# Later stores of converted weight tiles: five slots behind the operations that make them, tied to a product

## The chip, the cores and the metric

The kernel runs on one core of a Trainium2 chip. The metric is the device time of one execution in microseconds (us), as a median of runs. Five engines run side by side: TensorE (PE, matrix products; PEld is its weight load), VectorE (DVE), ScalarE (ACT), GpSimd (POOL) and SyncE (SP). SP computes nothing here. It issues almost all transfers between the chip's memory (HBM) and the on-chip memory, one after the other: its queue is in order, and an issue that has to wait for its data holds up everything queued behind it.

## What is computed

Eight batches of causal attention with two kinds of masks (four heads look at the last 32 positions, four at every 32nd position), then a feed-forward layer with the gate h * cos(h). All data are float32.

```python
scores = np.where(masks, scale * np.matmul(q, k.transpose(0, 1, 3, 2)), -1e9)   # (8, 8, 576, 576)
attn = np.exp(scores - np.max(scores, axis=-1, keepdims=True))
attn = attn / (np.sum(attn, axis=-1, keepdims=True) + 1e-09)
x = np.matmul(attn, v).transpose(0, 2, 1, 3).reshape(4608, 512)
h = x @ w_in                       # w_in 512 x 2048, float64 on input
g = h * np.cos(h)
return g @ w_out                   # w_out 2048 x 512, float64 on input
```

The weights arrive as 64-bit numbers, and the kernel itself turns them into 32-bit ones.

## The kernel before

There are two long stages. In the first, to about 490 us, the attention of batch b + 1 is worked in between the products of batch b with w_in, and h goes to HBM (`h_all`). In the second, h comes back in pairs of tiles, passes the gate and is multiplied by w_out. Every operand is split into a high and a low part, and a product of two is three products of parts.

**Slots.** The first stage has 8 x 56 slots of the program. The weights w_in stand as 8 blocks f, and a block in a batch is seven products by a scheme with seven in place of eight, in 7 slots (`STEP`); 8 blocks make the 56 slots of a batch (`PER_BATCH`). Each product is six matmuls (L532). A dictionary `plan` says which product is begun in which slot, `bursts` where units of attention are worked in, and `steps` what else is traced there. PE's order is written out by hand: `in_turn` orders each matmul behind the one before.

**What follows a product.** PE's results are combined in `hidden` (L550 on DVE, L548 on ACT) into a buffer of h, of which there are three (pool `hb`). When both halves are there, L552 stores the buffer with SP. By the order of the products a store of h falls to the slots 5 and 6 of every seven, one of each of two neighbouring blocks. So the stores come in pairs, and they tell in the timeline of SP which slot is being worked. A buffer is free again when its store has landed, and DVE works its queue in order: the operations of the next softmax stand behind an L550 that waits for a buffer.

**The conversion of w_out.** `whole_output_weights` treats tile n of 16. `land` (L156) loads 512 KB of 64-bit words into a tile `raw`, of which there are three. In slot 112 + 17 n, `to_float32` works it with two operations of ACT (L165, L169) and two of DVE (L170, L173) into the tile `sums`, of which there is one, and L583 stores that to `w_all` in HBM. `output_sums` treats the four pairs f = 1, 2, 4, 5 (`SEVEN`) in slots 112 + 17 (2 f + 2) and 8 later. It loads a pair of tiles of `w_all` into a tile of the ring `raw` (L602), makes four sums and differences of quarters in another tile of the ring with three operations of POOL (the last is L610), and stores them to `t_all` with L611. Later `output_weights` and `split_sums` read `w_all` and `t_all` back, split them and keep them for the second stage.

**Who sets the order.** A planner puts each engine's instructions in a row by a simulated course of the kernel: an instruction whose inputs and buffers are ready there is placed then. `with_product(i)` adds an edge without a semaphore: in the plan, instruction i comes no earlier than the last matmul that was traced before it. On the chip the tie itself makes nothing wait. Generators make the steps: `in_steps(work, *slots)` continues the generator `work` in each of the slots given, up to its next `yield`.

Of the kernel before, what the change touches and what calls it, by code (L numbers as in the profile page):

```python
# [100 lines left out]
def attention_cos_ffn(ctx, tc, qkl, vl, qkvs, w_in, w_out, eye, eye16, mask_l0, mask_l, mask_s, out):  # L101
    nc = tc.nc
# [19 lines left out]
    w_all = dram.tile([NFC, P, DM], F32, name="w_all")  # L122
    t_all = dram.tile([len(SEVEN), P, 2 * DM], F32, name="t_all")
# [9 lines left out]
    def order(later, first, reason):  # L133
        tc.add_manual_dep(
            later.ins, first.ins.name,
            mybir.DependencyInfo(mybir.DependencyClass.NoSync, mybir.DependencyReason.DATA), reason=reason,
        )
# [12 lines left out]
    def with_product(begun):  # L150
        if turn is not None:
            order(begun, turn, "with this product")

    def land(cv, src):
        raw = cv.tile([P, 512, 2], I32, name="raw", bufs=3)
        load = nc.sync.dma_start(out=raw.rearrange("p n w -> p (n w)"), in_=src)  # L156
        if len(loads) == UNITS:
            order(load, loads[-1], "units first")
        return raw

    def to_float32(raw, out, bits=None):
        low, top = raw[:, :, 0], raw[:, :, 1]
        scaled = top.bitcast(F32)
        bits = low if bits is None else bits
        with_product(nc.scalar.activation(  # L165
            out=bits, in_=low.bitcast(U32), func=AF.Copy, scale=2.0 ** -29 * (1.0 - 2.0 ** -16),
            bias=7.5 * 2.0 ** -16 - 0.5,
        ))
        with_product(nc.scalar.activation(out=scaled, in_=scaled, func=AF.Copy, scale=2.0 ** -112))  # L169
        nc.vector.scalar_tensor_tensor(  # L170
            out=bits, in0=top, scalar=-0x80000000, in1=bits, op0=ALU.bitwise_and, op1=ALU.bitwise_or
        )
        nc.vector.scalar_tensor_tensor(  # L173
            out=out, in0=top, scalar=3, in1=bits, op0=ALU.logical_shift_left, op1=ALU.bitwise_or
        )
# [402 lines left out]
    def whole_output_weights(cv, n):  # L578
        raw = land(cv, w_out.bitcast(I32)[n])
        yield  # L580
        t = cv.tile([P, 3, 2 * P], F32, name="sums")[:, :2].rearrange("p k n -> p (k n)")
        to_float32(raw, t.bitcast(I32))
        nc.sync.dma_start(out=w_all[n], in_=t)  # L583
        yield

    def output_weights(room, n, rest=nc.gpsimd):
# [8 lines left out]
    def whole_tile(cv):  # L595
        return cv.tile([P, 512, 2], I32, name="raw", bufs=3).bitcast(F32).rearrange("p n w -> p (n w)")

    def output_sums(cv, n):

        f = SEVEN[n]  # L600
        both = whole_tile(cv).rearrange("p (f n) -> p f n", f=2)
        nc.sync.dma_start(out=both, in_=w_all[2 * f:2 * f + 2].rearrange("f p n -> p f n"))  # L602
        yield
        b = both.rearrange("p f (j n) -> p (f j) n", j=2)
        t = whole_tile(cv).rearrange("p (j n) -> p j n", j=4)
        with_product(nc.gpsimd.tensor_tensor(
            out=t[:, :2], in0=b[:, 1:2].broadcast_to([P, 2, 2 * P]), in1=b[:, 0:4:3], op=ALU.subtract
        ))
        nc.gpsimd.tensor_tensor(out=t[:, 2], in0=b[:, 3], in1=t[:, 0], op=ALU.subtract)
        nc.gpsimd.tensor_tensor(out=t[:, 3], in0=b[:, 2], in1=t[:, 2], op=ALU.subtract)  # L610
        nc.sync.dma_start(out=t_all[n], in_=t.rearrange("p j n -> p (j n)"))  # L611
        yield

    def split_sums(room, n):
# [161 lines left out]
    with ExitStack() as phase:  # L776
        cv = phase.enter_context(tc.tile_pool(name="cv", bufs=1))
# [16 lines left out]
        m, n, o = ((pools[name], name) for name in "mno")  # L794
# [58 lines left out]
        def in_steps(work, *slots):  # L853
            work = iter(work)
            for slot in slots:
                steps.setdefault(slot, []).append(partial(next, work, None))

        for n in range(2, NF):
            for i in range(2):
                at = 7 * n + 7 * i // 2 - 13  # L860
# [2 lines left out]
            in_steps(weight_sums(cv, f), *(16 + 10 * f + i for i in (0, 2, 5, 7)))  # L863
        for n in range(NFC):
            at = 2 * PER_BATCH + 17 * n
            in_steps(whole_output_weights(cv, n), at - 10, at)
        for n in range(NFC - LATE):
            at = (B - 1) * PER_BATCH + STEP * (n // 2) + 12 + 3 * (n % 2)
            in_steps(output_weights(lambda: whole_tile(cv)[:, :DM], n), at - 6, at)
        for n, f in enumerate(SEVEN):  # L870
            at = 2 * PER_BATCH + 17 * (2 * f + 2)
            in_steps(output_sums(cv, n), at, at + 8)
        for n, at in enumerate(SUMMED):
            at += (B - 1) * PER_BATCH
            in_steps(split_sums(lambda: whole_tile(cv), n), at - 6, at, at + 4)
        for b in range(1, B):
            for i, (summed, made) in enumerate(PREPARED):
                at = (b - 1) * PER_BATCH
# [5 lines left out]
        for slot in range(max(*plan, *steps) + 1):  # L884
            b, at = divmod(slot, PER_BATCH)
# [149 lines left out]
```

## Time and profile before

| | |
|---|---|
| median of 3 runs | 871.63 us (871.21 to 871.90) |
| profiled execution | 872.13 us, its span 870.40 us |
| busy in the span | PE 98%, PEld 91%, DVE 64%, ACT 60%, POOL 60% |
| granted clock of TensorE | 1.00 (2.4 GHz) over the span |
| moved by DMA | 150.22 MB, 173 GB/s on average |

Times are in us from the start of the span. PE's matmuls overlap and their ends are modelled, so its busy share tells where it stood still rather than how near it is to its peak. "L552" is line 552 of the kernel. An entry of the timeline ends with the idle time before it and what ended that.

### The profile page before, as it was taken

What the parts mean: (1) busy time and instruction counts of PE and PEld (TensorE: products, weight loads), DVE (VectorE), ACT (ScalarE), POOL (GpSimd) and SP (SyncE); (2) the same over time, 40 slices, a digit from 0 to 9 for tenths busy, and PEclk for the clock granted to TensorE, in tenths of its full rate; (3) what the DMA queues carried; (4) which work ended last, traced back from release to release, by engine and by line L of the source; (5) the groups of instructions that cost most, each with busy time, mean ns of one, the idle gap of its engine ahead of it and who ended that gap; (6) DMA issues with size and microseconds to landing.
All of it is one profiled execution on the core that took longest, in us unless ns stands there. A gap on an engine that the chain in (4) does not pass through costs nothing.

```text
span 870.4 us, 22827 instructions
## 1 busy us (share of the span) xinstructions
PE 857.0 (98%) x9021; PEld 792.4 (91%) x9021; DVE 554.2 (64%) x1069; ACT 519.6 (60%) x1029; POOL 523.1 (60%) x514
## 2 busy tenths in 40 slices
PE   9899999999999999999999999999999999999998
PEld 5799899999999899999999889999999999999996
DVE  5888756658566566686433666666666666666661
ACT  3766444545345354453456887777777777777772
POOL 2578974416216134171166488888888888888851
PEclk9999999999999999999999999999999999999999
DMA  9698445554766666674355744444444444444430
GB/s 332 206 301 267 144 147 161 191 192 158 265 215 207 231 221 220 211 251 159 129 188 214 250 133 124 131 123 131 124 122 129 126 123 129 130 130 132 134 97 25
DMA packets 91339, 150.22 MB, mean 173 GB/s; under 512 B 8416, under 2 KB 52960, under 8 KB 91232
## 3 DMA queue, kind: packets, MB, share of 16 engines
q1 hardware_dynamic: 90512, 148.54, 52.6%
q8 instruction: 71, 1.16, 0.6%
q14 instruction: 36, 0.29, 0.1%
q10 hardware_dynamic: 720, 0.23, 0.1%
HBM read 95.25 MB, written 53.48 MB: 171 GB/s over the span
## 4 chain that ended last, share of the span: by engine, by line
PE 86%; DMA 4%; DVE 3%; POOL 3%; ACT 2%; issue 2%; SPq 0%; DVEq 0%; POOLq 0%; ACTq 0%
PE q L709 41%; PE m L532 18%; PE n L532 9%; PE m L503 5%; PE o L532 4%; PE acc L331 2%; PE acc L396 2%; PE acc L313 2%; DMA h_all<-h 1%; PE acc L366 1%; PE acc L383 1%; POOL x_lo L179 1%; POOL g_lo L179 1%; DMA both<-w_all 1%; DVE h L550 1%
## 5 line engine op out<-in xcount | busy, mean ns | idle before, releaser
L709 PE MATMUL q<-w,g_hi 128*128 128x512 f32 (+1 forms) x1028 | 215.6, 349 | 0.0
L709 PEld LDWEIGHTS q<-w,g_hi 128*128 128x128 f32 x1028 | 171.1, 189 | 25.5
L179 POOL TENSOR_TENSOR g_lo<-g,g_hi 128x896 fp32r<-128x896 f32 x64 | 135.2, 2134 | 0.2 <-ACT g_hi L178 0.2
L709 PE MATMUL q<-w,g_lo 128*128 128x512 f32 (+1 forms) x514 | 119.4, 349 | 0.3 <-POOL g_lo L179 0.3
L532 PE MATMUL m<-x_hi,w 128*128 128x288 f32 x448 | 109.8, 300 | 1.7 <-DVE h L550 1.0
L532 PE MATMUL m<-x_hi,v 128*128 128x288 f32 x448 | 108.8, 297 | 0.1
L657 ACT ACTIVATE wave<-r,quarter 128x512 f32<-128x512 f32 x144 | 98.6, 685 | 3.3 <-DVE r L655 3.2
L709 PEld LDWEIGHTS q<-w,g_lo 128*128 128x128 f32 x514 | 87.9, 189 | 12.9 <-POOL g_lo L179 0.5
L655 DVE SCALAR_TENSOR_TENSOR r<-wave,h_in 128x512 f32<-128x512 int32 x144 | 95.6, 681 | 4.5 <-ACT wave L654 3.0
L179 POOL TENSOR_TENSOR g_lo<-r,g_hi 128x512 fp32r<-128x512 f32 x44 | 57.1, 1298 | 65.6 <-PE q L709 50.5
L654 ACT ACTIVATE wave<-h_in 128x512 int32<-128x512 f32 x144 | 82.9, 590 | 0.4 <-DMA h_in<-h_all 0.4
L178 ACT CAST g_hi<-g 128x896 fp32r<-128x896 f32 x64 | 60.6, 947 | 36.7 <-PE q L709 29.9
L532 PEld LDWEIGHTS m<-x_hi,w 128*128 128x128 f32 x448 | 78.0, 188 | 3.5 <-DVE h L550 1.7
L532 PEld LDWEIGHTS m<-x_hi,v 128*128 128x128 f32 x448 | 78.0, 188 | 0.5 <-ACT m L540 0.4
L540 ACT COPY m<-m 128x288 f32<-128x288 f32 x112 | 44.6, 398 | 56.1 <-PE m L532 48.6
L283 POOL TENSOR_TENSOR pn_s<-e_sb,z 128x324 f32<-128x324 f32 x28 | 20.9, 746 | 87.2 <-DVE z L281 76.8
L283 POOL TENSOR_TENSOR e_sb<-e_sb,z 128x384 f32<-128x384 f32 x24 | 20.4, 851 | 86.3 <-DVE z L281 77.6
L709 PE MATMUL q<-v,g_hi 128*128 128x256 f32 x512 | 71.9, 283 | 0.0
L532 PE MATMUL m<-x_lo,w 128*128 128x288 f32 x224 | 66.1, 295 | 0.0
L532 PE MATMUL m<-x_lo,v 128*128 128x288 f32 x224 | 66.1, 295 | 0.0
L709 PEld LDWEIGHTS q<-v,g_hi 128*128 128x128 f32 x512 | 66.0, 192 | 0.0
L673 DVE TENSOR_TENSOR g<-wave,h_in 128x512 f32<-128x512 f32 x64 | 44.1, 689 | 28.7 <-ACT wave L657 26.8
(137 smaller groups left out, 2036.5 us busy)
## 6 DMA issues: line engine op xcount, KB each, us to landing
h_all<-h SPq DMA_DIRECT2D x128, 288.0 KB, 2.5
h_in<-h_all SPq DMA_DIRECT2D x144, 256.0 KB, 2.8
qk<-in_qkvs SPq DMA_DIRECT2D x28, 324.0 KB, 4.4
out<-o SPq DMA_DIRECT2D x35, 256.0 KB, 2.7
qk<-in_qkl SPq DMA_DIRECT2D x21, 416.0 KB, 4.4
raw<-in_w_in SPq DMA_DIRECT2D x16, 512.0 KB, 4.5
raw<-in_w_out SPq DMA_DIRECT2D x16, 512.0 KB, 5.2
v<-in_vl SPq DMA_DIRECT2D x24, 224.0 KB, 4.2
```

The source lines that it names most:

```text
L178: with_product(cast(out=hi, in_=x))
L179: return rest.tensor_tensor(out=lo, in0=x, in1=hi.bitcast(F32), op=ALU.subtract)
L283: nc.gpsimd.tensor_tensor(out=pn, in0=e, in1=z[:, :n].unsqueeze(2).broadcast_to([P, n, w]), op=ALU.mult)
L313: self.scored = self.pe(nc.tensor.matmul(s_ps[quarter_of(c), t * KW:(t + 1) * KW], q_t[half(j), p, QB * t:QB * (t + 1)], k_t[half(j), p, Q ...
L503: in_turn(nc.tensor.matmul(self.banks[i, j], a[:, c * P:(c + 1) * P], y[:, c], start=k == 0 and m == 0, stop=k == 1 and m == len(ops) - 1, ...
L532: in_turn(nc.tensor.matmul(bank, a[:, c * P:(c + 1) * P], y[:, c], start=first and i == 0, stop=i == len(ops) - 1, skip_group_check=True,))
L540: nc.scalar.copy(out=t, in_=self.bank[name[0]])
L654: with_product(nc.scalar.activation(out=k, in_=h, func=AF.Copy, scale=1.0 / (2.0 * math.pi), bias=0.25))
L655: nc.vector.scalar_tensor_tensor(out=r, in0=k, scalar=-2.0 * math.pi, in1=h, op0=ALU.mult, op1=ALU.add)
L657: sin = nc.scalar.activation(out=wave, in_=r, func=AF.Sin, bias=quarter)
L673: nc.vector.tensor_tensor(out=g[:, :4].rearrange("p n t -> p (n t)"), in0=wave, in1=h, op=ALU.mult)
L709: in_turn(nc.tensor.matmul(at, a, w, start=first, stop=True, skip_group_check=True))
```

## The change

Both stores get a step of their own: after a `yield`, tied to the last product that was traced when this step comes. The step of the w_all store is 5 slots behind that of the conversion. The step of the t_all store is 5 slots behind that of the sums, which itself stays where it was, 8 slots after slot 112 + 17 (2 f + 2), while the load of the pair moves by one slot.

```diff
@@ whole_output_weights
         to_float32(raw, t.bitcast(I32))
-        nc.sync.dma_start(out=w_all[n], in_=t)
+        yield
+        with_product(nc.sync.dma_start(out=w_all[n], in_=t))
         yield
@@ output_sums
         nc.gpsimd.tensor_tensor(out=t[:, 3], in0=b[:, 2], in1=t[:, 2], op=ALU.subtract)
-        nc.sync.dma_start(out=t_all[n], in_=t.rearrange("p j n -> p (j n)"))
+        yield
+        with_product(nc.sync.dma_start(out=t_all[n], in_=t.rearrange("p j n -> p (j n)")))
         yield
@@ the steps
         for n in range(NFC):
             at = 2 * PER_BATCH + 17 * n
-            in_steps(whole_output_weights(cv, n), at - 10, at)
+            in_steps(whole_output_weights(cv, n), at - 10, at, at + 5)
         for n, f in enumerate(SEVEN):
             at = 2 * PER_BATCH + 17 * (2 * f + 2)
-            in_steps(output_sums(cv, n), at, at + 8)
+            in_steps(output_sums(cv, n), at + 1, at + 8, at + 13)
```

## Rows read from the trace of the kernel before

**Rows 1.** Part 1 of the page: busy time of each engine, its share of the span, instructions.

```profile
PE 857.0 (98%) x9021; PEld 792.4 (91%) x9021; DVE 554.2 (64%) x1069; ACT 519.6 (60%) x1029; POOL 523.1 (60%) x514
```

**Rows 2.** The chain that ended last in order of time: start, length, what. The runs of 24 products of L396, one in each batch of the first stage from the second on.

```profile
121.63 0.84 PE acc L396 x24
...
178.74 0.84 PE acc L396 x24
...
236.63 0.84 PE acc L396 x24
...
294.48 0.84 PE acc L396 x24
...
352.87 0.84 PE acc L396 x24
...
409.91 0.84 PE acc L396 x24
```

**Rows 3.** The timeline of PE: start, length, line, operation, tiles, and in brackets the idle time before it and what ended it. The matmuls between 160 and 430 us for which it marks such a time.

```profile
209.71 0.40 PE L532 MATMUL m<-x_hi,w 128*128 128x288 f32 x1 [0.58 <-DVE h L550]
...
293.42 0.40 PE L532 MATMUL n<-x_hi,w 128*128 128x288 f32 x1 [1.22 <-DVE h L550]
...
351.81 0.40 PE L532 MATMUL n<-x_hi,w 128*128 128x288 f32 x1 [1.02 <-DVE h L550]
```

**Rows 4.** The timeline of DVE: one operation of the conversion of tile 3, and the last of that of tile 7.

```profile
207.36 1.93 DVE L170 SCALAR_TENSOR_TENSOR raw<-raw 128x512 int32<-128x512 int32 x1
...
276.31 0.85 DVE L173 SCALAR_TENSOR_TENSOR sums<-raw 128x512 int32<-128x512 int32 x1
```

**Rows 5.** The timeline of DVE: the four longest stops between 200 and 430 us that the landing of a store of h ended.

```profile
224.46 0.46 DVE L550 TENSOR_TENSOR h<-o,m 128x288 f32<-128x288 f32 x1 [2.24 <-DMA h_all<-h]
...
253.64 0.46 DVE L550 TENSOR_TENSOR h<-o,m 128x288 f32<-128x288 f32 x1 [3.04 <-DMA h_all<-h]
...
289.75 0.46 DVE L550 TENSOR_TENSOR h<-o,m 128x288 f32<-128x288 f32 x1 [3.94 <-DMA h_all<-h]
...
345.39 0.46 DVE L550 TENSOR_TENSOR h<-o,m 128x288 f32<-128x288 f32 x1 [2.84 <-DMA h_all<-h]
```

**Rows 6.** The chain that ended last in order of time: the two stores of h on it between 160 and 430 us (start, time to landing).

```profile
282.72 6.93 DMA h_all<-h
...
340.17 5.10 DMA h_all<-h
```

**Rows 7.** DMA issues by line: out<-in, engine, how many, KB each, median us from issue to landing.

```profile
h_all<-h SPq DMA_DIRECT2D x128, 288.0 KB, 2.5
...
raw<-in_w_out SPq DMA_DIRECT2D x16, 512.0 KB, 5.2
...
w_all<-sums SPq DMA_DIRECT2D x16, 256.0 KB, 2.2
...
t_all<-raw SPq DMA_DIRECT2D x4, 512.0 KB, 3.6
```

**Rows 8.** Waits of SP's queue: line, what it waited for, us in total, times, the longest.

```profile
SPq L583 <- DVE sums L173: 27.3, 11, 6.1
...
SPq L583 <- DVE z L281: 8.5, 3, 4.9
...
SPq L611 <- POOL raw L610: 6.0, 2, 5.4
...
SPq L602 <- DMA w_all<-sums: 4.3, 3, 1.6
```

**Rows 9.** The timeline of ACT: a copy that completes a buffer of h, and the first operation of the conversion of tile 7.

```profile
210.81 0.40 ACT L548 COPY h<-m 128x288 f32<-128x288 f32 x1 [0.60 <-PE m L532]
...
273.55 0.68 ACT L165 ACTIVATE raw<-raw 128x512 int32<-128x512 uint32 x1
```

**Rows 10.** The timeline of SP's queue: start, length, line, transfer, how many in a row (x2: two issues and the time between them).

```profile
211.56 0.38 SPq L552 DMA_DIRECT2D h_all<-h  x1
...
276.64 0.33 SPq L611 DMA_DIRECT2D t_all<-raw  x1
277.01 0.43 SPq L156 DMA_DIRECT2D raw<-in_w_out  x1
277.56 1.39 SPq L552 DMA_DIRECT2D h_all<-h  x2
279.06 0.42 SPq L583 DMA_DIRECT2D w_all<-sums  x1
279.55 2.07 SPq L156 DMA_DIRECT2D raw<-in_w_out  x2
...
282.72 2.15 SPq L552 DMA_DIRECT2D h_all<-h  x2
...
338.36 0.33 SPq L611 DMA_DIRECT2D t_all<-raw  x1
338.74 0.42 SPq L156 DMA_DIRECT2D raw<-in_w_out  x1
340.17 1.21 SPq L552 DMA_DIRECT2D h_all<-h  x2
```

**Rows 11.** Two stretches: start and end, length, busy time of each engine (and instructions), granted clock, DMA share, GB/s.

```profile
276.60:289.70 13.10, 13.10 (x217) 12.58 (x216) 4.79 (x12) 4.07 (x12) 1.88 (x3) 1.00 0.95 328
338.30:345.30 7.00, 7.00 (x137) 6.70 (x136) 2.52 (x7) 3.09 (x8) 0.76 (x2) 1.00 0.95 311
```

## The prediction

> **What bounds the kernel now.** First the busy shares: TensorE (PE) works through 98% of the span [rows 1], so time can only be won where PE stands still, and the change touches one stretch, from the first conversion of w_out to the last, about 158 to 419 us. Second the chain of work in order of time. The same run of 24 products of L396 comes round once per batch, so the distances between their starts are the lengths of the batches [rows 2]: 57.11, 57.89, 57.85, 58.39 and 57.04 us. The first and the last of these five hold conversions and stores too and still take 57.1, so 57.05 is the undisturbed length, and the three between lose 0.84 + 0.80 + 1.34 = 2.98 us. That is all that this stretch has to give: 0.34% of the kernel. Third the timeline of PE for the places of that loss [rows 3]: 0.58 us idle at 209.71, 1.22 at 293.42, 1.02 at 351.81, together 2.82 of the 2.98, each ended by L550 on VectorE (DVE).
>
> What made L550 late differs. At 209.71 DVE itself was slow: the conversion's L170, an operation of 512 elements per partition, took 1.93 us there [rows 4]; no store is in that chain. At 293.42 and 351.81 DVE stood for 3.94 and 2.84 us on "h_all<-h", that is, a buffer of h was not free because its store had not landed [rows 5]; the chain names those stores, issued at 282.72 and 340.17 and landed after 6.93 and 5.10 us [rows 6], where the median is 2.5 [rows 7]. Everything queued behind L550 on DVE, the softmax steps of the next unit among it, waits with it. So the path here is: a full DMA queue, a late h store, a blocked DVE, an idle PE. Not every block reaches PE: DVE stood 3.04 us before 253.64 and 2.24 before 224.46 [rows 5], and the timeline of PE marks no idle time at either.
>
> **What SP waits for.** The queue's own waits [rows 8] put 27.3 + 8.5 us on the stores of L583 and 6.0 on those of L611: SP stands at a store until DVE or GpSimd (POOL) has made its tile. These 41.8 us look like the prize and are not. SP does nothing but issue, so such a wait costs what stands behind it and is already due. After the longest of them, 6.1 us before 211.14, the next entry is an h store at 211.56 [rows 10], whose copy L548 began at 210.81 and took 0.40 [rows 9]: held for 0.35 us. After the 5.4 us before 276.64 comes a load of raw at 277.01 [rows 10]. Of the three buffers of raw one is t itself, one is under conversion until L173 ends at 277.16 [rows 4], so the load takes the third, the pair that the same POOL operations read, and could not go before them in any order.
>
> **The change, part by part.** (1) The 16 stores of w_all (256 KB each) and the 4 of t_all (512 KB) [rows 7] are tied to a product five slots after the step that makes their tile. No instruction is added or removed on any engine; the tie orders the plan alone and sets no semaphore. A batch of 56 slots takes 57.05 us, so a slot is 1.02 us and five are 5.1. But the old stores didn't issue at the step: they wait for the conversion, whose operations take some 3.6 us (the one that L583 stores at 279.06 ran from L165 at 273.55 to the end of L173 at 277.16 [rows 4, 9]). So a store moves by 5.1 - 3.6 = 1.5 us, or 2 with the spread of such times, in SP's plan, past one or two h stores or a pair of q/k and v loads, not by five slots.
>
> (2) Of the 41.8 us of waiting nearly all goes at the stores, yet where a load of raw stood right behind, it takes the wait over, since it needs the same tile free. Worth nothing on the path: 0, with 0 and -0.35 as ends (the time that the h store of 211.56 was held).
>
> (3) At 338.36 the t_all store, and at 338.74 a raw load, go into the queue just ahead of the pair of h stores at 340.17 [rows 10]. In the kernel's slots that pair is of 292 and 293, and the t_all store moves from 290 plus its operations to the product of 295: behind the pair. The queue was full in that stretch, 311 GB/s with the DMA engines 95% busy [rows 11], so 524,288 bytes fewer ahead of the h store are worth 524,288 / 311,000 = 1.69 us of its landing: 343.6 in place of 345.3. That is more than the 1.02 us PE lost there, so all 1.02 should go; ends 0 and -1.34 (that batch's whole excess). I take -1.0.
>
> The Trainium skill, "DMA: Bandwidth & Descriptors", section "Queues, rings and completion order", says that all DMAs that SP issues share one row of rings and each engine consumes a ring in order. The rows agree, an h store taking 2.5 us at the median and 6.93 behind loads, and it speaks against this change: bytes are moved in the queue, none is taken out. By the same page's limit of 358 GB/s (section "Specifications") the 512 KB would be an estimated 1.46 us instead of 1.69, and the sum the same.
>
> (4) The stop before 293.42 should stay. Ahead of the h store of 282.72 stand, from 276.64 on, t_all, three loads of raw, two h stores and one of w_all [rows 10], in a stretch 95% busy at 328 GB/s [rows 11]. After the change t_all is tied to slot 227 and w_all to slot 236, and that h store belongs to the product of 236 and needs its result copied first: both are still ahead. SP still can't pass 276.6, since the raw load there needs POOL's tile. The same bytes from the same start: 0, with ends -1.22 (a raw load slips behind the h store) and +0.8 (another 256 KB gets ahead: 262,144 / 328,000).
>
> (5) The four loads of a pair of w_all tiles (L602) wait for the landing of the store (4.3 us of SP's waits already, [rows 8]), and the raw loads that take their buffer in turn follow them. They shift by the same 1.5 to 2 us. Nothing needs their data at once: the pair is used a dozen microseconds later. But a megabyte, 3.3 us at 311 GB/s, moves closer to other h stores. Ends 0 and +1.22 (the dearest stop shown) at one place; I take +0.3. Moving L602 by one slot keeps its place behind the conversion of the same slot: 0.
>
> (6) Ring of raw tiles: t is held until a store that issues about 2 us later has landed. The next raw loads run many slots ahead of their conversions, so 0. The tile "sums" is written next 12 slots after the moved store: 0. The stage behind 430 us is untouched: 0.
>
> **Sum.** The profiled execution took 872.13 us, its span of 870.40 and 1.73 around it: 872.13 - 1.0 + 0.3 = 871.4. That execution is 0.50 above the median of the runs, 871.63; against the median it is 870.9.
>
> **The rivals.** R1, both jams go: the t_all store, and with its later landing one or two raw loads, fall behind the h store of 282.72 as well. Then 1.22 + 1.02 = 2.24 go, 869.4; with the whole excess of the three batches 868.65. For it: the 6.93 us hang on an order of SP that the plan may well reshuffle. Against: step 4, equal bytes from an equal start. Chance 0.20.
>
> R2, slower: the jam moves to other h stores. The stores now stand directly ahead of the h store of the same product in several cases (slots 117, 236 and 321), and L602 with its raw load ahead of a pair that had them further off. It decides from where DVE is stopped for about 3 us: 2.84 and 3.94 cost PE 1.02 and 1.22, 3.04 cost nothing [rows 3, 5]. Two new such stops with the old ones left: 871.63 + 2 x 1.22 = 874.1. Against: at 3.3 us per megabyte a jam clears within half of the 7 slots (7.1 us) from one pair of h stores to the next, so it must hit them exactly. Chance 0.14.
>
> R3, nothing: the raw loads take over the waits, the t_all store stays ahead of the pair of 340.17 because the plan runs ahead of the chip, and the same bytes stand in the same places: 871.6. Chance 0.21.
>
> My forecast, one of two stops gone and a little given back, has 0.45, with 870.2 to 871.5 as its own range.
>
> **How the numbers follow.** 0.2% (1.74 us) is about what a measurement of this kernel can tell from no change. Below 869.9 lie nearly all of R1 and a small tail of the forecast: 0.23. Above 873.4 lies most of R2, with the shuffling of other queues that no row prices: 0.13. The rest, 0.64, is within. For 8 in 10 the range reaches into R1 and towards R2: 869.0 to 872.9.
>
> **What would show it.** SP's waits at the two store lines should fall from 41.8 us to under 10, with waits at the raw loads' line rising. The t_all store near 338 should come after the h pair, whose first store then lands within about 3.5 us, and the batch of 58.39 us should shorten to about 57.3. The batch with the stop at 293 should stay at 57.85, and the idle time at 209.7 should stay. I'm wrong if a new idle time of PE of a microsecond appears behind a stop of DVE on h_all (R2), if the stop at 293 goes (R1), or if the time moves outside this stretch.

## The result and the profile after

| | before | after |
|---|---|---|
| median | 871.76 us (6 runs, 871.21 to 872.65) | 877.49 us (6 runs, 876.88 to 883.13) |
| profiled execution | 872.13 us, span 870.40 | 877.40 us, span 875.6 |
| PE busy | 857.0 us | 857.7 us |

The change makes the kernel slower: ratio 1.0082, 95% interval 1.0064 to 1.0101. Two executions among the experiments below, the profiled one of the w_all part alone and one of the t_all part alone, ran at a granted clock of 0.66 and took 1175 and 1176 us, and stand in none of the medians and ratios. PE has the same work, so the 5.2 us of span are time in which it stood still or ran slowly. The marks of [rows 2] tell where: in the chain in order of time of the changed kernel (start, length, what) the same runs of L396 stand at

```profile
120.92 0.84 PE acc L396 x24
...
178.01 0.84 PE acc L396 x24
...
241.36 0.84 PE acc L396 x24
...
299.13 0.84 PE acc L396 x24
...
358.01 0.84 PE acc L396 x24
...
415.58 0.84 PE acc L396 x24
```

So the batches take 57.09, 63.35, 57.77, 58.88 and 57.57 us, against 57.11, 57.89, 57.85, 58.39 and 57.04 before. One batch is 5.46 us longer and the last two some 0.5 each; the first mark stands 0.71 us earlier than before, and another half microsecond comes back behind the last.

In that batch the timelines of PE and of DVE and the chain show one new stop of PE, at a place where DVE already stood before (2.24 us, [rows 5]) and PE next to nothing. PE and DVE of the changed kernel (last column: idle time before, and what ended it):

```profile
229.47 0.43 PE L532 MATMUL m<-x_hi,v 128*128 128x288 f32 x1 [4.12 <-ACT m L540]
```

```profile
227.70 0.46 DVE L550 TENSOR_TENSOR h<-o,m 128x288 f32<-128x288 f32 x1 [6.22 <-DMA h_all<-h]
```

The chain there (start, length, what):

```profile
217.98 9.60 DMA h_all<-h
...
228.16 0.41 DVE e_sb L276
...
228.66 0.04 ACT e_sb L277
...
229.04 0.39 ACT m L540
...
229.47 1.63 PE m L532 x6
231.10 1.44 PE o L532 x6
232.54 1.10 PE acc L331 x48
```

It is the mechanism of [rows 5, 6] at a third place: a store of h, of slot 173, lands after 9.60 us, and DVE can't begin L550 nor the softmax step L276 behind it. ACT's L277 waits for L276, and behind L277 in ACT's queue stands the copy L540 that empties the bank `m` for which PE waits. Then a second loss follows: PE begins again at half clock. Busy times in the window behind the stop (start and end, length, PE, PEld, DVE, ACT, POOL, granted clock, DMA share, GB/s):

```profile
229.40:235.00 5.60, 5.53 (x112) 5.12 (x113) 3.22 (x9) 0.94 (x4) 3.42 (x4) 0.70 0.34 118
```

A mean of 0.70 is a stretch at the lower of the two levels (1.2 GHz) after four idle microseconds, and then the upper again. The same three groups took 1.06, 0.79 and 0.83 us before; two of them in the chain of the kernel before:

```profile
226.22 1.06 PE m L532 x6
...
228.08 0.83 PE acc L331 x48
```

So the clock cost 0.57 + 0.65 + 0.27 = 1.49, and 4.12 + 1.49 = 5.61 us is the batch's loss within 0.15.

PE did lose a little at this place before. The timeline of PE marks idle time only above 0.15 us, but these two neighbours in the kernel before leave 0.14 between them (225.79 + 0.29 = 226.08):

```profile
225.79 0.29 PE L532 MATMUL m<-x_hi,w 128*128 128x288 f32 x1
226.22 0.40 PE L532 MATMUL m<-x_hi,v 128*128 128x288 f32 x1
```

So DVE stood 2.24 us for 0.14 of PE before, and 6.22 for 4.12 after: 2.10 us of slack both times.

What stands ahead of the late store is told by SP's queue. Before:

```profile
214.79 0.32 SPq L552 DMA_DIRECT2D h_all<-h  x1
215.20 0.39 SPq L602 DMA_DIRECT2D raw<-w_all  x1
215.64 0.49 SPq L156 DMA_DIRECT2D raw<-in_w_out  x1
216.22 0.38 SPq L358 DMA_DIRECT2D v<-in_qkvs  x1
216.70 0.38 SPq L303 DMA_DIRECT2D qk<-in_qkl  x1
218.26 1.41 SPq L552 DMA_DIRECT2D h_all<-h  x2
```

After:

```profile
210.51 3.87 SPq L552 DMA_DIRECT2D h_all<-h  x2
214.43 0.42 SPq L584 DMA_DIRECT2D w_all<-sums  x1
214.95 0.40 SPq L358 DMA_DIRECT2D v<-in_qkvs  x1
215.44 0.40 SPq L303 DMA_DIRECT2D qk<-in_qkl  x1
216.97 0.38 SPq L603 DMA_DIRECT2D raw<-w_all  x1
217.41 0.47 SPq L156 DMA_DIRECT2D raw<-in_w_out  x1
217.98 0.96 SPq L552 DMA_DIRECT2D h_all<-h  x2
```

The w_all store of tile 3 moved from 211.14 behind the h stores of slots 166 and 167. The load of the first pair reads that tile, so it waits for the landing (2.5 us, to 216.9), and the raw load takes its buffer behind it. The megabyte that left at 215.2 to 215.6 now leaves at 217.0 to 217.4, half a microsecond ahead of the h store, and the moved store's 256 KB are new ahead of it as well. The two loads of v and qk (L358, L303) stand ahead of the h store in both kernels; they only changed places with the megabyte.

The waits of SP (us in total, times, longest) against [rows 8]:

```profile
SPq L613 <- POOL raw L611: 5.4, 1, 5.4
...
SPq L603 <- DMA w_all<-sums: 4.3, 3, 1.6
SPq L156 <- DMA t_all<-raw: 4.0, 2, 3.8
SPq L584 <- DVE sums L173: 3.8, 4, 1.9
SPq L584 <- DVE z L281: 3.2, 1, 3.2
SPq L156 <- DVE sums L173: 2.1, 1, 2.1
```

The waits at the two store lines (L613 and L584) fell from 41.8 to 12.4 us, which is what the edit does by itself; the two rows of the raw loads (L156) hold 6.1 us. No time came of it.

### The profile page after: what moved, and what is told of

Its sections match the earlier page's. It is cut to its first block, busy times and chain, and to the rows that moved or that the text cites. A ratio compares the mean times of both kernels' runs of the same rounds, so it can differ in the third digit from the quotient of the medians.

```text
span 875.6 us, 22827 instructions
## 1 busy us (share of the span) xinstructions
PE 857.7 (98%) x9021; PEld 793.2 (91%) x9021; DVE 553.8 (63%) x1069; ACT 519.9 (59%) x1029; POOL 523.1 (60%) x514
## 4 chain that ended last, share of the span: by engine, by line
PE 84%; DMA 6%; DVE 4%; ACT 2%; issue 2%; POOL 2%; SPq 0%; DVEq 0%; ACTq 0%; POOLq 0%
PE q L711 43%; PE m L532 16%; PE n L532 8%; PE m L503 5%; PE o L532 4%; DMA h_all<-h 4%; PE acc L331 2%; PE acc L396 2%; PE acc L313 1%; PE acc L366 1%; POOL x_lo L179 1%; DVE h L550 1%; PE acc L383 1%; DMA w_all<-sums 1%; DMA v<-in_qkl 1%
## 5 line engine op out<-in xcount | busy, mean ns | idle before, releaser
L711 PE MATMUL q<-w,g_hi 128*128 128x512 f32 (+1 forms) x1028 | 215.6, 349 | 0.0
L711 PEld LDWEIGHTS q<-w,g_lo 128*128 128x128 f32 x514 | 88.0, 189 | 12.4
L540 ACT COPY m<-m 128x288 f32<-128x288 f32 x112 | 44.6, 398 | 56.4 <-PE m L532 48.8
```

The lines of the kernel that those rows point to most:

```text
L540: nc.scalar.copy(out=t, in_=self.bank[name[0]])
L711: in_turn(nc.tensor.matmul(at, a, w, start=first, stop=True, skip_group_check=True))
```

## The experiments

**Theory A:** the late store of tile 3, through the pair load and the raw load chained behind its landing, puts a megabyte directly ahead of one h store. **Rivals:** the t_all stores or the moved pair loads do it (B); many small shifts add up (C); the late store's own bytes, or reading them back at once (D). Each group of four ran on one chip beside the kernel before, whose medians there were 872.16, 872.26 and 871.85 us.

**Parts of the change.** First only the w_all stores: in `output_sums` and its steps everything as before.

```diff
-        yield
-        with_product(nc.sync.dma_start(out=t_all[n], in_=t.rearrange("p j n -> p (j n)")))
+        nc.sync.dma_start(out=t_all[n], in_=t.rearrange("p j n -> p (j n)"))
...
-            in_steps(output_sums(cv, n), at + 1, at + 8, at + 13)
+            in_steps(output_sums(cv, n), at, at + 8)
```

> The change with its w_all part alone: the 16 stores of w_all five slots later and tied, the t_all stores and the loads of the pairs as before. Theory A (the store of tile 3, tied behind the pair of h stores of slots 166 and 167, drags the pair load and a raw load, 1 MB chained behind its landing, directly ahead of the h store of slot 173, which then lands after 9.6 us instead of 6.1; DVE stands for 6 us, PE empties and its clock drops): all of the loss stays, 876.5 to 877.5 us, and the batch with that store takes about 63.3 us instead of 57.9. Theory B (the t_all stores or the pair loads moved by one slot do it): 871.5 to 872.5. Theory C (many small shifts of all 20 stores): about half to three quarters of the loss, 874 to 876, spread over the batches.

Measured: 878.02 us (the median of three executions), ratio 1.0069 (1.0043 to 1.0095). Only the time is read, without a batch length. The loss is whole with the w_all part alone.

Then only the t_all stores and the pair loads, with the w_all stores as before:

```diff
-        yield
-        with_product(nc.sync.dma_start(out=w_all[n], in_=t))
+        nc.sync.dma_start(out=w_all[n], in_=t)
...
-            in_steps(whole_output_weights(cv, n), at - 10, at, at + 5)
+            in_steps(whole_output_weights(cv, n), at - 10, at)
```

> The change with its t_all part alone: the four t_all stores five slots behind the sums and tied, the pair loads one slot later; the w_all stores as before. Theory A: the store of tile 3 and the loads behind it are where they were, so the batch from 179 to 237 us takes 57.9 us; time 871.3 to 872.8. Theory B: 876 to 877.5. Theory C: 872.5 to 874.

Measured: 872.42 us, ratio 1.0002 (0.9990 to 1.0014), and the batch takes 57.47 us (178.73 to 236.20). B falls: this part costs nothing that can be told.

**One store of twenty.** The whole change with tile 3 put back, and the kernel before with tile 3 alone moved (there with `n == 3`, and `at + 5` for that tile only):

```diff
-        yield
-        with_product(nc.sync.dma_start(out=w_all[n], in_=t))
+        if n != 3:
+            yield
+        store = nc.sync.dma_start(out=w_all[n], in_=t)
+        if n != 3:
+            with_product(store)
...
-            in_steps(whole_output_weights(cv, n), at - 10, at, at + 5)
+            in_steps(whole_output_weights(cv, n), at - 10, at, *(() if n == 3 else (at + 5,)))
```

> The whole change, but the store of tile 3 alone (of 16) is issued where it was, behind its conversion and untied. Theory A: one store of twenty takes the large loss away: the h store of slot 173 lands after about 6 us, DVE stands about 2 us there, the batch falls from 63.3 to about 57.9, and the time to 872 to 873 (what is left is 0.5 us in each of the two batches from 299 to 416). Theory C: one twentieth to a tenth of the loss goes, 876.5 to 877.3.

> The kernel before, with the store of tile 3 alone delayed by five slots and tied; the other 19 stores as before. Theory A: this one store makes nearly the whole loss, 876 to 877.5, with a batch of about 63 us. Theory C: within 0.5 us of the kernel before, 871.3 to 872.3.

Tile 3 put back: 874.96 us, ratio 1.0032 (1.0015 to 1.0049). The batch fell to 57.47 us (178.59 to 236.06), its h store of slot 173 lands after 5.3 us, but the time stayed 2 us above what A said. Tile 3 alone: 876.05 us, ratio 1.0040 (1.0023 to 1.0057). Its ten executions lie between 873.09 and 878.64; the profiled one took 878.5 and is among the slowest. It has a batch of 64.15 us (178.87 to 243.02) and the same stop in the timelines of PE and of DVE:

```profile
230.24 0.61 PE L532 MATMUL m<-x_hi,v 128*128 128x288 f32 x1 [4.05 <-ACT m L540]
...
228.47 0.46 DVE L550 TENSOR_TENSOR h<-o,m 128x288 f32<-128x288 f32 x1 [6.15 <-DMA h_all<-h]
```

So one store makes most of the loss, and A as stated was too narrow: something else of the w_all part costs about 2 us. The run with tile 3 put back shows it in SP's queue, 140 us later:

```profile
356.94 0.37 SPq L606 DMA_DIRECT2D raw<-w_all  x1
357.36 0.46 SPq L156 DMA_DIRECT2D raw<-in_w_out  x1
357.92 0.85 SPq L552 DMA_DIRECT2D h_all<-h  x2
```

The last pair's load, behind the late store of tile 11, stands ahead of the h stores of slots 306 and 307 in the same way. The first of them lands after 7.0 us there, where it took 4.0 before, with a median of 2.5 [rows 7]. So both were put back (in the line of the steps too):

```diff
-        if n != 3:
+        if n not in (3, 11):
```

> The whole change, but two of its twenty stores, those of tiles 3 and 11 of w_all, are issued where they were. They are the second tiles of the first and the last pair, whose loads the late stores pushed against h stores. Theory A (only the stores that a pair load waits for cost): within 1 us of the kernel before, 871.5 to 873. Theory C (the other 18 cost too): 873.5 to 875.

Measured: 872.84 us, ratio 1.0010 (0.9998 to 1.0022); the two h stores land after 5.8 and 4.0 us. Two of twenty stores make the loss: about 4 us by tile 3 alone (876.05 - 872.16), and about 2 by tile 11 (2.8 us above the kernel before with tile 3 put back, 1.0 with both, on two chips). The other 18 make none that can be told.

**The chain behind the store, and the place.** Here the late stores stay as the change has them. In the first run the pair load is tied to its own product, in the second it reads another pair, which has long been stored:

```diff
-        nc.sync.dma_start(out=both, in_=w_all[2 * f:2 * f + 2].rearrange("f p n -> p f n"))
+        with_product(nc.sync.dma_start(out=both, in_=w_all[2 * f:2 * f + 2].rearrange("f p n -> p f n")))
```

```diff
-        nc.sync.dma_start(out=both, in_=w_all[2 * f:2 * f + 2].rearrange("f p n -> p f n"))
+        nc.sync.dma_start(out=both, in_=w_all[2 * f - 2:2 * f].rearrange("f p n -> p f n"))
```

> The whole change, and the four loads of pairs are tied to the product of their slot too, so that the pair load and the raw load that follows it come behind the h stores of slots 173 and 174 and behind the next pair of q/k and v loads; the stores of w_all and t_all stay where the change puts them, and the orders of PE, ACT and POOL are the same. Theory A (the megabyte dragged behind the store's landing is what the h store of slot 173 waits for): that h store lands within 4 us, PE has no stop near 229 us, and the time falls from 877.5 to 871.5 to 873.5, if no other h store is hit. Theory D (the late store of tile 3 itself, 256 KB, or its reading back at once, does it): no change, 876.5 to 878.

> The whole change, but the four pair loads read the pair of w_all before their own (tiles 2f-2 and 2f-1 instead of 2f and 2f+1), which is in HBM long before; so the sums of four pairs are made of other tiles. They no longer wait for the landing of the late store, and the plan issues them as soon as a buffer is free. Theory A: the stop near 229 us goes, since the pair load leaves at about 191 us and the raw load ahead of slot 166; 871.5 to 873.5. Theory D: the store of tile 3 keeps its place, so the stop stays, 876.5 to 878.

Pair load tied: 873.43 us, ratio 1.0018 (1.0005 to 1.0031). Other pair: 872.19 us, ratio 1.0004 (0.9994 to 1.0015). SP's queue in the first of them, where the pair load follows the h stores:

```profile
217.19 0.43 SPq L584 DMA_DIRECT2D w_all<-sums  x1
217.71 0.40 SPq L358 DMA_DIRECT2D v<-in_qkvs  x1
218.20 0.40 SPq L303 DMA_DIRECT2D qk<-in_qkl  x1
220.29 1.41 SPq L552 DMA_DIRECT2D h_all<-h  x2
...
224.26 0.38 SPq L603 DMA_DIRECT2D raw<-w_all  x1
```

The store of tile 3 is where the change puts it, and the h store of slot 173 lands after 2.2 us in this run and 2.4 in the other, not 9.6. The h store of slot 306, which the late store of tile 11 had hurt, lands after 2.9 and 3.5. D falls: neither the moved 256 KB nor the delay costs, the megabyte in the wrong place does. With the pair load tied some 1.2 us of loss are left. In its profiled execution (877.09 us, the slowest of ten) the last pair load and a raw load now stand ahead of the h stores of slots 313 and 314, which land after 8.1 and 8.4 us, and PE stands 0.55 and 0.51 us behind them.

The sharpest form is a later store. Tile 3 alone, as above with `n == 3`, but moved by 12 slots in place of 5:

```diff
-                in_steps(whole_output_weights(cv, n), at - 10, at)
+                in_steps(whole_output_weights(cv, n), at - 10, at, *((at + 12,) if n == 3 else ()))
```

> The kernel before, with the store of tile 3 alone delayed, as in the earlier run of that store, but by 12 slots instead of 5, to the product of slot 175, so that in SP's queue the pair load follows the h store of slot 173. Theory A (what counts is what stands ahead of that h store): later is cheaper than late, the h store of slot 173 lands after less than 5 us, no stop of PE of over 1 us near 229, 871.5 to 873.5. Theory E (the delay itself costs, the later the store the more): 877 to 880.

Measured: 872.3 us, ratio 1.0010 (0.9999 to 1.0021), against 1.0040 for five slots. In its queue the pair load at 221.89 follows the h store at 219.66, which lands after 2.9 us. It leaves as soon as the store of tile 3, issued at 217.54, has landed (4.3 us), so reading the bytes back at once is not what costs either, and E falls. A stop of DVE, 3.70 us before 232.48, still cost PE 0.84.

**Around the ring.** The stores of h of batches 1 to 7 in ACT's queue, in both kernels (`nc.scalar.dma_start` at L552):

> The whole change, and the 112 stores of h of batches 1 to 7 are issued by ACT's queue instead of SP's, so that they don't stand behind the loads in SP's row of rings. Theory A (a stop comes from an h store that is behind a megabyte in the same ring): the h stores land in 2 to 4 us through the jams, DVE doesn't stop on them for over 2 us, the stop near 229 us goes, and the time is 870 to 873, unless ACT's own issues (0.3 us each, and waits for DVE at its head) cost more. If the memory's own bandwidth or a slow engine of the 16 sets the landing and not the ring, h stores still land after 6 to 9 us there: 876 to 878.

> The kernel before with the stores of h in ACT's queue. Theory A: the two stops of PE at 293 and 352 us, 1.22 and 1.02 us, go with the late h stores, so 869.5 to 870.5, if ACT's own issues cost nothing; if ACT's waits at its head delay the copies that PE needs, slower, 873 to 880.

Measured: 875.35 us, ratio 1.0036 (1.0023 to 1.0048), and 874.04 us, ratio 1.0021 (1.0012 to 1.0031). The h store of slot 173 lands after 5.1 us in the first and PE has no stop near 229, so the other queue helps the changed kernel by about half of its loss; but the kernel before is 1.8 us slower by it, for a reason that was not looked into. With the stores of h in ACT's queue the change costs 1.3 us (875.35 against 874.04) in place of 5.1 to 5.7, which agrees with A. But 5.1 us to landing in a queue without those loads is not the 2 to 4 that were expected, so the order within one queue is not all of it.

**The change again,** on the chip of the last group:

> The changed kernel once more, beside the others on one chip. All theories: 876.5 to 878 with some executions above 880 where the lowered clock lasts longer; the stop near 229 us again, with an h store that lands after 9 to 10 us.

Measured: 876.95 us, ratio 1.0063 (1.0048 to 1.0078). The same h store lands after 7.7 us, less than expected, and the batch takes 59.94. PE and DVE there:

```profile
229.99 0.40 PE L532 MATMUL m<-x_hi,v 128*128 128x288 f32 x1 [2.21 <-ACT m L540]
...
228.23 0.46 DVE L550 TENSOR_TENSOR h<-o,m 128x288 f32<-128x288 f32 x1 [4.31 <-DMA h_all<-h]
```

Both profiles of the change have the stop, and its size differs. That this execution took 877.04 us all the same is in part an accident: its first mark stands at 123.36, 1.73 us later than in the kernel before and ahead of everything the change touches, with a granted clock of 0.57 from 34 to 38 us (1.00 there in the kernel before). So one profile tells where time goes, and the medians tell how much.

**A version that beats both.** If crowds of loads ahead of h stores are what costs, the loads should be tied, not the stores. The kernel before, with the lines below (the condition picks the loads of w_out from those of w_in):

```diff
         load = nc.sync.dma_start(out=raw.rearrange("p n w -> p (n w)"), in_=src)
+        if len(wi) == NF and len(wi[-1]) == 7:
+            with_product(load)
...
-        nc.sync.dma_start(out=both, in_=w_all[2 * f:2 * f + 2].rearrange("f p n -> p f n"))
+        with_product(nc.sync.dma_start(out=both, in_=w_all[2 * f:2 * f + 2].rearrange("f p n -> p f n")))
```

> The kernel before with its stores untouched and the loads tied instead: the 512 KB loads of w_out to the product of the slot where the program asks for them, 10 slots ahead of the conversion, and the pair loads to theirs, so that no two or three of them come in a row. Theory A: the crowd of t_all and three raw loads ahead of the h store of 282.72 is gone, one of the two stops of PE goes or both, 869.5 to 871. If the loads in their new slots meet other h stores: 872 to 876.

Measured: 870.0 us, ratio 0.9979 (0.9969 to 0.9988). Where three raw loads stood at 277 to 281 [rows 10], there is one:

```profile
277.53 0.33 SPq L613 DMA_DIRECT2D t_all<-raw  x1
277.96 1.14 SPq L554 DMA_DIRECT2D h_all<-h  x2
...
281.27 0.48 SPq L156 DMA_DIRECT2D raw<-in_w_out  x1
283.01 2.38 SPq L554 DMA_DIRECT2D h_all<-h  x2
```

Its h store at 283.01 lands after 5.1 us (6.93 before), that at 340.33 after 3.8 (5.10). The batches take 57.11, 57.48, 56.94, 57.29 and 57.02 us: of the 2.98 us that the three middle batches lost, 0.56 are left.

## Why the prediction was wrong, point by point

**What bounds the kernel** was right, and all later readings rest on it: a full queue, a late h store, a stopped DVE, an idle PE. With the loads tied 2.42 of the 2.98 us came back, so those were the doing of the loads' place. The 0.58 us of idle time at 209.7 stayed (at 208.98 in the changed kernel), as forecast.

**Step 1** was wrong in size for the stores that mattered. Measured from the mark of their batch, eight of the sixteen w_all stores did not move (0.4 us at most), and the others moved by 2.3 to 5 us in place of 1.5 to 2: that of tile 3 by 4.0 (211.14 - 178.74 before, 214.43 - 178.01 after), that of tile 11 by about 5. Both went past one pair of h stores, as forecast.

**Step 2** was right: 29 of 41.8 us of waiting went (12.4 are left, where under 10 was forecast), and no time came of it.

**Step 3 failed.** The t_all store did not fall behind the pair of slots 292 and 293. In the changed kernel

```profile
343.01 0.33 SPq L156 DMA_DIRECT2D raw<-in_w_out  x1
343.39 0.42 SPq L613 DMA_DIRECT2D t_all<-raw  x1
344.78 1.25 SPq L552 DMA_DIRECT2D h_all<-h  x2
```

it only changed places with the raw load, and the pair is still behind both. I counted slots as if a tie to slot 295 meant a place behind the h stores of 292 and 293. It needn't: tile 3's store, tied to slot 168, did go behind the h store of 167, and this one didn't. What the plan saw there no run shows. R3 had named the outcome, with the plan running ahead of the chip as its reason. The -1.0 did not come: the first h store lands after 5.7 us there (5.10 before), and the batch takes 58.88 us.

**Step 4** was right: the stop at 293 stayed (1.13 us at 298.07, batch 57.77).

**Step 5 is where the sum broke.** I saw that the pair loads wait for the landing and that the raw loads follow them, and that the megabyte comes closer to other h stores, and I priced it at +0.3 with +1.22 as the upper end, "at one place". It was two places and about 4 and 2 us, the 5.7 us of the change. (A megabyte at 311 GB/s is 3.4 us, not 3.3; nothing hangs on it.) The bound came from the dearest stop in the trace, but a stop isn't bounded by its like elsewhere. What PE loses is DVE's stop less a slack, and the slack belongs to the place. At this place it is 2.10 us in four profiles (2.24 of DVE for 0.14 of PE before, 6.22 for 4.12 and 4.31 for 2.21 in the two of the change, 6.15 for 4.05 with tile 3 alone). At the two stops that the prediction names it is 3.94 - 1.22 = 2.72 and 2.84 - 1.02 = 1.82 (in the changed kernel 3.84 - 1.13 = 2.71, and 3.34 less two stops of 0.48 and 1.03, 1.83), and where 3.04 us cost nothing it is at least that. So there is no common mark of "about 3 us", as R2 had it, and what I took for slack at 224, no idle time marked, was a stop that had already used its slack up: from there each microsecond of DVE costs one of PE, and the clock can come on top.

The trace before was enough for a better price. With the prediction's own shift of 1.5 to 2 us, and 256 KB more at the 311 GB/s of [rows 11], 0.84 us, the stop is 4.6 to 5.1 us, and PE loses 2.5 to 3.0 of it (an estimate). Measured from the mark of its batch the pair load in fact moved by 2.5 us (215.20 - 178.74 before, 216.97 - 178.01 after).

**Step 6** was right in time: raw loads do wait for a t_all store to land now (4.0 us, 3.8 at the longest), but the t_all part alone cost nothing that can be told.

**R2** was the right rival. Of the two forms that it named, the stores directly ahead of an h store cost nothing that can be told, and the pair load with its raw load was the cause, twice, at up to three times the price that I gave a stop (4 and 2 us for 1.22). Its 0.14 looks too low: four of the sixteen w_all stores are the last that a pair load waits for, and one of these loads stood ahead of a stop that had used up its slack. The range ended at 872.9; R2's own 874.1 would have been too low as well.

The sentence on ring order from the Trainium skill ("DMA: Bandwidth & Descriptors", "Queues, rings and completion order") agrees with these runs: by the order of one queue the same store lands after 2.2 to 9.6 us. I cited it against the change and did not let it move the sum. The 358 GB/s that the prediction took from the same page ("Specifications") was passed here: the kernel before moved 397 GB/s from 222 to 224 us.

## What to carry to other kernels

A store that a later load reads back is not a leaf: moving it moves every load that waits for its landing, and everything that takes buffers in turn behind that. Price such a move by the consumer at the end of the chain that is nearest to stalling already: take its stop in the trace, add the shift and the bytes, and take off the slack of that place, rather than taking another stop as the bound. The slack can be read where the bottleneck engine already loses a little, and the little may lie below what a timeline marks. And where bursts in a queue hurt small urgent stores, tie the big loads to the pace of the work, not the stores.

## What was not expected of the hardware

The landing of the h store of slot 173 ended long after most of the DMA work was done. In the changed kernel, by windows of one microsecond (last two columns: DMA share and GB/s):

```profile
226.00:227.00 1.00, 0.00 (x0) 0.00 (x0) 0.00 (x0) 0.00 (x0) 0.00 (x0) 1.00 0.21 84
227.00:228.00 1.00, 0.00 (x0) 0.00 (x0) 0.30 (x1) 0.00 (x0) 0.00 (x0) 1.00 0.07 28
```

A share of 0.07 is about one engine of 16. The trace holds more on it: a store raises its semaphore sixteen times, and the times are there. For this store the fifteenth came at 225.57 us and the last at 227.58, 2.01 us behind; with tile 3 alone they came at 225.28 and 228.35, 3.07 apart; in the second profile of the change at 227.88 and 228.11, only 0.23 apart. So the place of the megabyte explains a landing after about 7.6 us, and one late part made it 9.6. Without that part PE's stop in the first profile would have been about 2.1 us, as it was in the second (an estimate: 4.12 - 2.01). Which engine it was, and why it was late, no run here tells; so how much of the loss of about 4 us is due to such late parts in the other executions stays open.

The stops of PE of 4.12 and 4.05 us were followed by a lower granted clock (0.70 from 229.40 to 235.00 us, and 0.53 from 230.20 to 236.00 with tile 3 alone). The one of 2.21 us was not: there the granted clock from 229 to 235 us is 1.00.
